# A gated mix of linear attention and expert lookup: when the output weights are split, when tile 0 is counted, and the order of work in the pairs

## The chip, the cores and the metric

The kernel runs on one core of a Trainium2 chip. The metric is device time in microseconds (us) of one execution. The engines are TensorE (PE, matmuls; PEld its weight loads), VectorE (DVE), ScalarE (ACT), GpSimd (POOL) and SyncE (SP, which issues DMA transfers). Each engine works through its own queue in order; semaphores make it wait for others.

## The reference

For S = 2048 tokens x of width D = 512 the result is g a + (1 - g) b, with g = sigmoid(x . gate_w).

```
# a: linear attention, H = 32 heads of 16
q, k, v = split(x @ wqkv)
phi(y) = [softmax(y @ w_phi), softmax(-(y @ w_phi))]       # per head, 32 features
kv = sum_s phi(k)^T v ;  z = sum_s phi(k)
a  = (phi(q) kv / (phi(q) . z + 1e-6)) @ wo
# b: 256 experts = 16 x 16 keys, one expert per head
q1, q2 = halves of x @ w_q                                 # per head
e  = 16 * argmax(q1 @ k1^T) + argmax(q2 @ k2^T)
b  = sum over heads of gelu(x . u[e]) * v[e]               # softmax over one candidate is 1
```

Since every head of a token picks one of the same 256 experts, the kernel counts for each token how often each expert was picked and computes b as (count * gelu(x u^T)) @ v.

## The kernel before

**Tiles and precision.** The tokens are 16 tiles of 128 (NT = 16). All large matmuls run on pairs high + low of a rounded number: xh and xl for x, wah/wal, wbh/wbl, eh/el and so on for the weights; a product takes three matmuls (high high, high low, low high). High parts are casts (mostly ACT: x_high, L152), low parts are subtractions (x_low, L156, on DVE; Sums.low, L189, and join_end, L315, on POOL).

**Order.** The order on every engine is written by hand: the program is written in one sequence, and each engine executes its part of that sequence in order.

**First phase, keys and values.** Tiles 0 to 4 go one at a time: kproj and vproj (PE), the feature softmax (k_diffs on DVE, L115 to L121; k_exp on ACT, L267; k_sum on DVE, L271 and L272; k_mult on POOL, L276), and kvacc (PE, L283), which adds up kv and z in PSUM. From tile 5 the tiles go in pairs t = 5, 7, 9, 11, 13 with n = t + 1. For a pair the key and value projections are computed with seven block products (prod, L453) in the manner of Strassen; these need sums of the two tiles' inputs (Sums.add on POOL, L175 to L178; Sums.high on ACT; Sums.low, which writes gl and a second xl on POOL, L189). Intermediate banks are copied (pu, pv, and pk at L530: an ACT copy, which TensorE then adds on to).

In the same phase the score weights are built: score multiplies one head's wq (loaded by SP, 1 MB each, L143 and L421) with the keys (PE), and after each second head score_planes copies the result in two 16-bit planes (ACT) and SP transposes them by DMA (L299). The join puts them together again (join_tp and join_end on ACT; sl, the low part, on POOL, L315). After the last pair, tile 15 is done alone, and fold_q folds w_phi into the query weights, which come as rawq (SP).

**Second phase, queries and output.** First the sum z of the features is spread: zsum (ACT L914, POOL L915), its high and low part (t1h by ACT, t1l by DVE, L926, two arrays of the first phase that have become free), and two pairs of matmuls (z, L898 and L899), which ACT copies to zb. Then a loop over a = 0 to 14 works on four tiles at a time, n = a + 1 (scores front_s on PE; best, the argmax masks on DVE, L706 and L707; turn_eq, SP's transpose of the masks, et), a (softmax of the queries: soft_in on DVE, soft_exp on ACT L657, soft_w, the products with zb on POOL L663, soft_sum and soft_y, the sums on DVE L667 and L677, soft_b, the scales on DVE L685 to L692 and the multiplication by them on POOL L698), b = a - 1 (planes on ACT L730, transposes by SP, join on ACT L740, the count on DVE) and z = a - 2 (mid_num, the attention output oT on PE L749; num_lo; c_join and cl, the split of count times gelu, L849; back, the output matmuls po on PE, L861 and L868; store).

The count of a tile starts with mid_mask (PE, mk, from the transposed masks) and then takes some twenty small DVE steps: a prefix or (L776 to L780), two xors (L784, L786), and a bit count by shifts and adds (L794 to L805) up to the counts cf (L808). It is a Python generator; step(t, n) issues n of its steps and drain(t) the rest, so that they lie between other DVE work. Gelu parts are gelu_in (POOL L625), gelu_act (ACT L629 to L631), gelu_out (POOL L635); coef (POOL L812) multiplies the counts with gelu, and c_planes (ACT L817) and an SP transpose turn the product.

**The output weights** wo are four blocks of 128 rows. Before, they are loaded in the second phase (wo_load), cast on ACT (L980) and subtracted on POOL (L1006): blocks 0 and 1 at a = 0 into t1h and t1l, behind their use for z; blocks 2 and 3 at a = 1 into wbh and wbl, which hold the value weights until then.

Of the kernel before, what the change touches and what calls it, by code (L numbers as in the profile page):

```python
# [35 lines left out]
def mix_kernel(ctx, tc, xT, wqT, wkT, wv, wphi, wo, wq, kk, ug, ev, cst, out):  # L36
# [131 lines left out]
    class Sums:  # L168
# [11 lines left out]
        @staticmethod  # L180
        def high(t):
            for i in range(2):
                act.copy(Sums.h[i][0], rawx[t + 1 - i])
# [208 lines left out]
    def score(n, planes=True):  # L392
        nonlocal done
        for _ in range(n):
            score_w(done, raws[done])
            done += 1
            if not 4 < done < 9:
                load_wq()
# [11 lines left out]
    for t in range(5):  # L410
# [20 lines left out]
        if t == 3:  # L431
# [3 lines left out]
            Sums.low(5)  # L435
        if t < 4:
            k_exp(t)
            k_sum(t)
# [24 lines left out]
    for t in range(5, NT - 1, 2):  # L463
# [42 lines left out]
        if t == 5:  # L506
# [3 lines left out]
            join_all()  # L510
# [6 lines left out]
        score(1)  # L517
        if t == NT - 3:
            rawq = stage(wqT, "rawq")
        score(1)  # L520
# [10 lines left out]
        if t == 5:  # L531
            k_exp(t)
            k_sum(t)
            act.copy(vn, by16(e))
# [7 lines left out]
        if t + 3 < NT:  # L542
            Sums.high(t + 2)
# [4 lines left out]
        for u in more if n < NT - 4 else ():  # L548
            x_high(u)
# [301 lines left out]
    woh = [(t1h if k < 2 else wbh)[:, k] for k in range(NK)]  # L851
    wol = [(t1l if k < 2 else wbl)[:, k] for k in range(NK)]
# [40 lines left out]
    zh, zl = (m.rearrange("p k d -> p (k d)") for m in (t1h, t1l))  # L893

    def z_final():
        for s_ in halves:
            o = tr_bank("z")
            pe.matmul(o, neg, zh[:, s_], start=True, stop=False)  # L898
            pe.matmul(o, neg, zl[:, s_], start=False, stop=True)  # L899
            act.copy(zb[:, s_], o)  # L900

    def wo_load(ks):
        for k in ks:
            rawo[k] = w3.tile([P, D], F32, tag="ot", name=f"rawo{k}")
            sp.dma_start(rawo[k], wo[:, k, :])

    rawo = {}
    kvacc(NT - 2)
    act.copy(zc, acc[:, :, F])
    neg = w2.tile([P, P], F32R, name="neg", bufs=1)  # L910
# [14 lines left out]
    act.copy(zh, zsum)  # L925
    dve.tensor_tensor(zl, zsum, zh, op=ALU.subtract)  # L926
    soft_exp(0)
    front_s(1, 0)
    mid_mask(0)
    z_final()  # L930
    gelu_rest(0)
    wo_load((0, 1))
# [11 lines left out]
    for a in range(NT - 1):  # L944
# [6 lines left out]
        if a == 2:  # L951
            gelu_pre(a)
        if B:
            planes(b, 0)
            if Z:
                c_join(z)
            planes(b, 1)
            front_q(a)
        if owed:
            back(z - 1, owed)  # L960
            store(z - 1)
        if a == 1:
# [183 lines left out]
```

## Time and profile before

| | |
|---|---|
| median of three runs | 376.97 us (376.39 to 377.11) |
| the profiled execution, its own time | 376.26 us |
| its span in the profile | 374.5 us |
| granted TensorE clock | 1.0 |
| busy: PE, PEld, DVE, ACT, POOL | 365.2, 285.7, 334.1, 256.7, 206.3 us |
| instructions in the trace | 8838 |

Times within the trace count from the start of the span. Instructions of one engine overlap at their ends, so two that follow each other directly can add up to more than the time between their starts; for matmuls of 128x512 the step from one to the next is what counts. In a row of the timeline the columns are start, duration, engine, line, operation, output<-input, shapes, number merged, and in brackets the idle time of the engine just before and what ended it. In a row of the waits they are the waiting operation, what it waited for, the sum in us, the number of times and the longest.

### The profile page before, as it was taken

To read this page: it belongs to the slowest core of one execution; us is meant where nothing else is said; L and a number is where in the kernel's file an instruction comes from. 1 tells how busy PE (TensorE), PEld (TensorE's weight loads), DVE (VectorE), ACT (ScalarE), POOL (GpSimd) and SP (SyncE) were. 2 spreads that over 40 slices of the span, in tenths; PEclk is the share of its full clock that TensorE was granted. 3 is DMA by queue.
4 is the path that set the end of the run, shared out by engine and by line. 5 is a ranking of instruction groups with operands and counts; after the bars stand their busy time and mean duration, and the time that the engine had idled before them with its cause. 6 is when DMAs were issued, how large, how long until landed. Compare 5 with 4: busy or idle time off the path is not lost.

```text
span 374.5 us, 8838 instructions
## 1 busy us (share of the span) xinstructions
PE 365.2 (98%) x3443; PEld 285.7 (76%) x3443; DVE 334.1 (89%) x784; ACT 256.7 (69%) x458; POOL 206.3 (55%) x206
## 2 busy tenths in 40 slices
PE   8999999999999998999999999999999999999995
PEld 4766776667878886778888878888778888888875
DVE  4679898999877989999999999999999999999993
ACT  5576678776576674878759568677786787687741
POOL 1089989799838745844535427335445454454700
PEclk9999999999999999999999999999999999999999
DMA  7967887757981124244253242453553532532201
GB/s 273 330 243 244 302 273 188 255 170 196 265 184 35 21 68 112 45 87 97 71 86 87 70 98 60 98 80 35 113 60 82 114 70 72 115 63 65 72 31 56
DMA packets 72218, 46.67 MB, mean 125 GB/s; under 512 B 63600, under 2 KB 64496, under 8 KB 69872
## 3 DMA queue, kind: packets, MB, share of 16 engines
q1 hardware_dynamic: 71312, 45.24, 47.0%
q10 hardware_dynamic: 864, 0.87, 0.8%
q8 instruction: 27, 0.44, 0.5%
q14 instruction: 15, 0.12, 0.1%
HBM read 26.43 MB, written 4.19 MB: 82 GB/s over the span
## 4 chain that ended last, share of the span: by engine, by line
PE 76%; DVE 7%; ACT 5%; issue 4%; DMA 3%; POOL 3%; POOLq 0%; ACTq 0%; DVEq 0%
PE po L861 10%; PE s L56 6%; PE s L57 6%; PE s L58 6%; PE po L868 5%; PE pq L56 4%; PE pk L453 3%; PE pq L58 3%; PE pq L57 3%; PE ws L292 3%; PE oT L749 2%; PE pu L453 2%; PE kvacc L283 2%; PE pp L57 2%; PE pp L58 2%
## 5 line engine op out<-in xcount | busy, mean ns | idle before, releaser
L663 POOL TENSOR_TENSOR w<-d,zb 128x512 f32<-128x512 f32 x32 | 41.0, 1297 | 78.3 <-ACT d L657 78.3
L56 PE MATMUL s<-sh,xh 128*128 128x512 f32 x128 | 50.8, 397 | 0.0
L57 PE MATMUL s<-sl,xh 128*128 128x512 f32 x128 | 49.9, 390 | 0.0
L58 PE MATMUL s<-sh,xl 128*128 128x512 f32 x128 | 49.8, 389 | 0.0
L698 POOL TENSOR_TENSOR d<-d,st 128x512 f32<-128x512 f32 x30 | 31.2, 1063 | 27.6 <-DVE st L692 25.6
L657 ACT ACTIVATE d<-d 128x512 f32<-128x512 f32 x32 | 20.1, 634 | 32.9 <-DVE d L119 24.8
L276 POOL TENSOR_TENSOR d<-d,st 128x1024 f32<-128x1024 f32 x16 | 33.6, 2101 | 13.3 <-DVE st L272 9.3
L740 ACT COPY pt<-tp 128x1024 uint16<-128x1024 uint16 x28 | 36.3, 1366 | 0.0
L730 ACT COPY pl<-d 128x1024 uint16<-128x1024 uint16 x28 | 29.2, 1045 | 9.1 <-POOL d L698 9.1
L58 PEld LDWEIGHTS s<-sh,xl 128*128 128x128 f32 x128 | 24.0, 188 | 5.0
L56 PEld LDWEIGHTS s<-sh,xh 128*128 128x128 f32 x128 | 24.0, 188 | 4.7
L57 PEld LDWEIGHTS s<-sl,xh 128*128 128x128 f32 x128 | 24.1, 188 | 4.6
L56 PE MATMUL pq<-wah,xh 128*128 128x512 f32 x64 | 26.8, 418 | 0.0
L58 PE MATMUL pq<-wah,xl 128*128 128x512 f32 x64 | 25.1, 392 | 0.0
L57 PE MATMUL pq<-wal,xh 128*128 128x512 f32 x64 | 25.0, 390 | 0.0
L271 DVE TENSOR_REDUCE st<-d 128x64 f32<-128x1024 f32 x16 | 19.4, 1212 | 5.1 <-ACT d L267 4.9
L707 DVE TENSOR_TENSOR eq<-s,mx 128x512 bf16<-128x512 f32 x32 | 22.1, 692 | 1.1
L667 DVE TENSOR_REDUCE st<-d 128x32 f32<-128x512 f32 x32 | 21.6, 683 | 1.6
L267 ACT ACTIVATE d<-d 128x1024 f32<-128x1024 f32 x16 | 17.0, 1065 | 7.6 <-DVE d L121 7.6
L156 DVE TENSOR_TENSOR xl<-xr,xh 128x512 fp32r<-128x512 f32 (+2 forms) x17 | 20.7, 1239 | 1.5 <-ACT xh L152 1.4
L706 DVE TENSOR_REDUCE mx<-s 128x32 f32<-128x512 f32 x32 | 21.8, 682 | 0.0
L677 DVE TENSOR_REDUCE st<-w 128x32 f32<-128x512 f32 x32 | 20.5, 677 | 0.6 <-POOL w L663 0.5
(258 smaller groups left out, 1119.9 us busy)
## 6 DMA issues: line engine op xcount, KB each, us to landing
wq<-wq SPq DMA_DIRECT2D x16, 1024.0 KB, 5.6
xr<-xT SPq DMA_DIRECT2D x15, 256.0 KB, 3.9
y<-ot SPq DMA_DIRECT2D x15, 256.0 KB, 2.3
rawk<-wkT SPq DMA_DIRECT2D x1, 1024.0 KB, 6.0
rawq<-wqT SPq DMA_DIRECT2D x1, 1024.0 KB, 6.7
rawo<-wo SPq DMA_DIRECT2D x4, 256.0 KB, 3.7
rawu<-ug SPq DMA_DIRECT2D x2, 258.0 KB, 4.2
rawv<-wv ACTq DMA_DIRECT2D x2, 256.0 KB, 4.5
```

The lines of the kernel that those rows point to most:

```text
L56: pe.matmul(o, ah, bh, start=(first and i == 0), stop=False)
L57: pe.matmul(o, ah, bl, start=False, stop=False)
L58: pe.matmul(o, al, bh, start=False, stop=(last and i == n - 1))
L276: pool.tensor_tensor(g64(d), g64(d), b64(st[:, 128:192]), op=ALU.mult)
L663: pool.tensor_tensor(hs(e["w"], i), hs(e["ph"], i), hs(zb, i), op=ALU.mult)
L667: dve.tensor_reduce(pair(e["st"][:, 64:128])[:, :, i], hs(e["ph"], i), axis=AX.X, op=ALU.add)
L698: eng.tensor_tensor(g64(d)[:, gs_], g64(d)[:, gs_], r[:, gs_].unsqueeze(2).to_broadcast([P, 32, F]), op=ALU.mult)
L706: dve.tensor_reduce(mx, p3, axis=AX.X, op=ALU.max)
L707: dve.tensor_tensor(e["eq"][:, 512 * half:512 * half + 512].rearrange("p (h f) -> p h f", f=F), p3, mx.unsqueeze(2).to_broadcast([P, H, F] ...
L730: act.copy(pl, e["ph"][:, halves[i]].bitcast(U16).rearrange("p (c j) -> p j c", j=2))
L740: act.copy(p16[:, :, 4 * i:4 * i + 4, :], e["tp"][i].rearrange("p (j g) n -> p j g n", j=2))
L861: pe.matmul(po, a, b, start=(i == 0), stop=False)
```

## The change

It moves work and renames where it is stored; the matmuls and their order on TensorE stay as they are.

- **Output weights.** Blocks 0 and 1 are loaded before tile 15's work into buffers of the x tiles that are spare, cast on ACT (L593) and subtracted on POOL (L594) before the last k_mult. Blocks 2 and 3 come as one 512 KB load behind kvacc of tile 14. Block 2 is split at the start of the second phase into gh and gl (POOL L945), block 3 at a = 1 into the halves of wbh and wbl (POOL L988). zh and zl become two halves each, in buffers that the later transposes use.
- **Count of tile 0.** At a = 0 only the first six steps are issued (up to the xors), and best(1, 0), best(1, 1) and turn_eq(1) come before soft_y(0); soft_b(0) has no count steps in between. At a = 1 six steps come in one piece behind soft_in(1), best(2, 0) before soft_sum, and the rest of the count behind soft_sum; vproj of tile 15 and its copy, and gelu_act(1), are moved as well.
- **Pairs.** The transposes of the score planes are issued before the next loads of wq instead of behind them, and rawq behind the last of them. x_low(7) moves to tile 3, x_low(9) behind k_exp(5), the other x_low behind k_diffs(behind); x_high(9), Sums.high(7) in part, join_end(2) and score_planes(3) move around the copy pk of t = 5.

The lines behind the change in the file have other numbers: what was L663, L667, L677 is L679, L683, L693; the count's L784, L786, L794, L797 to L802 are L800, L802, L810, L813 to L818; L849, L861, L868 are L865, L877, L884.

```diff
@@ pairs
             Sums.low(5)
+            x_low(7)
...
-        for u in (t + 2, t + 3):
-            if u < NT - 1:
-                x_low(u)
         if behind:
             k_diffs(behind)
+        for u in (t + 2, t + 3):
+            if u < NT - 1 and u not in (7, 9):
+                x_low(u)
...
             k_mult(4)
-            join_all()
+            x_high(9)
...
+            join_tp(j2, tp, tj2)
...
-        score(1)
+        score(2, t > 5)
+        if t > 5:
+            load_wq()
+            load_wq()
         if t == NT - 3:
             rawq = stage(wqT, "rawq")
-        score(1)
...
         act.copy(d, b)
         if t == 5:
+            join_end(j2, tj2)
+            score_planes(3)
             k_exp(t)
+            x_low(9)
             k_sum(t)
+            Sums.high(7, (0,))
@@ tile 15
+    rawo = {k: spare(wo[:, k], f"rawo{k}", [P, D]) for k in range(2)}
...
+    for k in range(2):
+        act.copy(t1h[:, k], rawo[k])
+        pool.tensor_tensor(t1l[:, k], rawo[k], t1h[:, k], op=ALU.subtract)
     k_mult(t)
@@ second phase
+    zh, zl = ([w3.tile([P, 512], F32R, tag=tag, name=f"{n}{i}") for i in range(2)] for n, tag in (("zh", "pl"), ("zl", "tp")))
+    for i, s_ in enumerate(halves):
+        act.copy(zh[i], zsum[:, s_])
+        dve.tensor_tensor(zl[i], zsum[:, s_], zh[i], op=ALU.subtract)
     soft_exp(0)
+    act.copy(woh[2], rawo[2])
+    pool.tensor_tensor(wol[2], rawo[2], woh[2], op=ALU.subtract)
...
+        gelu_in(a)
         if a == 1:
-            v15 = vproj(NT - 1)
-        gelu_in(a)
+            pool.tensor_tensor(wol[3], rawo[3], woh[3], op=ALU.subtract)
...
         if B:
-            soft_in(a, dealt(a, b, z))
-            drain(b)
+            if a == 1:
+                for _ in gate(a):
+                    pass
+                soft_in(a)
+                step(b, 6)
+            else:
+                soft_in(a, dealt(a, b, z))
+                drain(b)
...
         soft_w(a)
+        if a == 1:
+            best(n, 0)
         soft_sum(a, 0)
         soft_sum(a, 1)
+        if a == 1:
+            drain(b)
         if a == 0:
-            step(a, 8)
-        if a < 2:
-            for k in (2 * a, 2 * a + 1):
-                pool.tensor_tensor(wol[k], rawo[k], woh[k], op=ALU.subtract)
+            step(a, 6)
+        if a != 1:
+            best(n, 0)
         if a == 0:
-            wo_load((2, 3))
-        best(n, 0)
+            best(n, 1)
+            turn_eq(n)
...
-        soft_b(a)
-        best(n, 1)
-        turn_eq(n)
+        if a == 0:
+            soft_b(a, lambda t: None)
+        else:
+            soft_b(a)
+            best(n, 1)
+            turn_eq(n)
```

On VectorE, from the writing of tile 0's scales (the last step of soft_b) to the sums of tile 1 (st is the softmax's scratch, pq the query projection, X and T the count's scratch, mx and eq the argmax), the order before is:

```order
L692 SCALAR_TENSOR_TENSOR st_1750<-st_1750,gs_1768 128x32 x2
L802 TENSOR_TENSOR T_1862<-X_1861 128x256
L706 TENSOR_REDUCE mx_1_1890<-s_1_1821 128x32
L707 TENSOR_TENSOR eq_1871<-s_1_1821,mx_1_1890 128x512
L115 TENSOR_REDUCE st_1940<-pq_1911 128x32
L621 RECIPROCAL gs_1895<-gs_1895 128x1
L803 TENSOR_SCALAR X_1861<-T_1862 128x128
L804 TENSOR_SCALAR T_1862<-T_1862 128x128
L805 TENSOR_TENSOR X_1861<-X_1861,T_1862 128x256
L808 TENSOR_TENSOR cf_1946<-X_1861 128x256
L117 TENSOR_REDUCE st_1940<-pq_1911 128x32
```

and now, from the same place:

```order
L708 SCALAR_TENSOR_TENSOR st_1760<-st_1760,gs_1778 128x32 x2
L637 RECIPROCAL gs_1892<-gs_1892 128x1
L115 TENSOR_REDUCE st_1941<-pq_1900 128x32
L117 TENSOR_REDUCE st_1941<-pq_1900 128x32
L119 TENSOR_TENSOR d_1940<-pq_1900,st_1941 128x32x16
L121 TENSOR_TENSOR d_1940<-st_1941,pq_1900 128x32x16
L810 TENSOR_TENSOR X_1946<-m_1869,m_1870 128x256
L813 TENSOR_SCALAR T_1947<-X_1946 128x256
L814 TENSOR_TENSOR X_1946<-X_1946,T_1947 128x512
L815 TENSOR_SCALAR T_1947<-X_1946 128x256
L816 TENSOR_SCALAR X_1946<-X_1946 128x256
L817 TENSOR_TENSOR X_1946<-X_1946,T_1947 128x512
```

Before, the count of tile 0 was all but done by the end of tile 1's softmax differences; now six of its steps stand together behind them.

On GpSimd, from the first gelu step of tile 0 to the products of tile 1 (w), the order before is:

```order
L625 TENSOR_TENSOR x_1806<-x_1806,px_1805 128x256
L663 TENSOR_TENSOR w_1847<-d_1749,zb 128x32x16 x2
L1006 TENSOR_TENSOR t1l<-rawo_1810,t1h 128x512
L1006 TENSOR_TENSOR t1l<-rawo_1812,t1h 128x512
L698 TENSOR_TENSOR d_1749<-d_1749,st_1750 128x512 x2
L625 TENSOR_TENSOR x_1899<-x_1899,px_1898 128x256
L663 TENSOR_TENSOR w_2047<-d_1939,zb 128x32x16 x2
```

and now, with the split of block 2 ahead of it:

```order
L945 TENSOR_TENSOR gl<-rawo_1719,gh 128x512
L641 TENSOR_TENSOR x_1824<-x_1824,px_1823 128x256
L679 TENSOR_TENSOR w_1859<-d_1759,zb 128x32x16 x2
L714 TENSOR_TENSOR d_1759<-d_1759,st_1760 128x512 x2
L641 TENSOR_TENSOR x_1896<-x_1896,px_1895 128x256
L988 TENSOR_TENSOR wbl<-rawo_1719,wbh 128x512
L679 TENSOR_TENSOR w_2044<-d_1940,zb 128x32x16 x2
```

Two subtractions have left the stretch between products and multiplications of tile 0, one now stands ahead of the products of tile 1.

On VectorE, around tiles 3 and 4 and the first pair (xr is a raw tile), the order before is:

```order
L189 TENSOR_TENSOR gl<-xr_284,gh 128x512
L271 TENSOR_REDUCE st_439<-d_438 128x64
L272 RECIPROCAL st_439<-st_439 128x64
L115 TENSOR_REDUCE st_530<-pk_516 128x32
L117 TENSOR_REDUCE st_530<-pk_516 128x32
L119 TENSOR_TENSOR d_529<-pk_516,st_530 128x32x16
L121 TENSOR_TENSOR d_529<-st_530,pk_516 128x32x16
L156 TENSOR_TENSOR xl_68<-xr_359,xh_65 128x512
L156 TENSOR_TENSOR xl_68<-xr_397,xh_65 128x512
```

and now:

```order
L189 TENSOR_TENSOR gl<-xr_284,gh 128x512
L156 TENSOR_TENSOR xl_68<-xr_359,xh_65 128x512
L271 TENSOR_REDUCE st_439<-d_438 128x64
L272 RECIPROCAL st_439<-st_439 128x64
L115 TENSOR_REDUCE st_531<-pk_517 128x32
L117 TENSOR_REDUCE st_531<-pk_517 128x32
L119 TENSOR_TENSOR d_530<-pk_517,st_531 128x32x16
L121 TENSOR_TENSOR d_530<-st_531,pk_517 128x32x16
L156 TENSOR_TENSOR xl_68<-xr_397,xh_65 128x512
```

x_low(7), the subtraction on xr_359, now stands between gl and the sums of tile 3.

More of the change, by code (lines that the diff above doesn't have):

```diff
@@ L180, in high @@
         @staticmethod
-        def high(t):
-            for i in range(2):
+        def high(t, which=(0, 1)):
+            for i in which:
                 act.copy(Sums.h[i][0], rawx[t + 1 - i])
@@ L396, in score @@
             done += 1
[L397 removed]
+            if done < 5:
                 load_wq()
@@ L849, in back_cl @@
         eng.tensor_tensor(cl, o[:, :2 * P], ch, op=ALU.subtract)
-    woh = [(t1h if k < 2 else wbh)[:, k] for k in range(NK)]
-    wol = [(t1l if k < 2 else wbl)[:, k] for k in range(NK)]
+    woh, wol = ([a[:, 0], a[:, 1], b.rearrange("p k n -> p (k n)"), c[:, 0]]
+                for a, b, c in ((t1h, gh, wbh), (t1l, gl, wbl)))
     def back_mm(t, cols=slice(0, D), bank=None):
```

49 lines of the change are left out of this document (27 added, 22 removed).

## The prediction

> **What bounds the kernel now.** I read first the busy times of the page, then the table by stage, then PE's waits.
>
> ```profile
> PE 365.2 (98%) x3443; PEld 285.7 (76%) x3443; DVE 334.1 (89%) x784; ACT 256.7 (69%) x458; POOL 206.3 (55%) x206
> ```
>
> ```profile
> 150.00:155.00 5.00, 4.65 (x40) 3.73 (x39) 4.86 (x10) 4.94 (x10) 4.82 (x4) 1.00 0.27 51
> ```
>
> ```profile
> PE mk L768 <- DMA et<-eq: 1.6, 1, 1.6
> PE pk L453 <- ACT pk L530: 1.0, 2, 0.6
> PE oT L749 <- ACT pt L740: 0.7, 1, 0.7
> ```
>
> TensorE is busy for 98% of the span. The change leaves its matmuls and their order as they were, so all that can be won is the idle time that is left. That lies in two zones: the pairs (45 to 80 us) and the start of the second phase (130 to 163 us). For the second, the row 150 to 155 (columns PE, PEld, DVE, ACT, POOL) says more than the waits do: VectorE 4.86 of 5 us, ScalarE 4.94, GpSimd 4.82. All are full at once. The end of that zone is in the timeline of TensorE and VectorE:
>
> ```profile
> 162.28 0.40 PE L868 MATMUL po<-el,ch 128*128 128x512 f32 x1
> 162.52 0.72 PE L868 MATMUL po<-eh,cl 128*128 128x512 f32 x2
> ```
>
> ```profile
> 162.03 0.42 DVE L849 TENSOR_TENSOR cl<-ctj,ch 128x256 fp32r<-128x256 f32 x1
> ```
>
> Cl of tile 0 is ready at 162.45, and TensorE takes it at 162.52, one pitch (0.23) behind the matmul before. TensorE, having lost 3 us on the way, arrives just when VectorE is done. If its waits go and VectorE is no earlier, it waits here.
>
> **The change, first zone (pairs).**
>
> ```profile
> 70.16 0.39 PE L453 MATMUL pv<-wbh,xl 128*128 128x512 f32 x1
> 71.14 0.50 PE L453 MATMUL pk<-sh,xh 128*128 128x512 f32 x1 [0.59 <-ACT pk L530]
> ...
> 74.26 0.39 PE L453 MATMUL pe<-t1l,gh 128*128 128x512 f32 x1
> 74.75 0.50 PE L453 MATMUL pe<-t1h,gl 128*128 128x512 f32 x1
> ...
> 76.00 0.40 PE L453 MATMUL pu<-ul,xh 128*128 128x512 f32 x1
> 76.46 0.50 PE L453 MATMUL pu<-uh,xl 128*128 128x512 f32 x1
> ```
>
> Matmuls of this form follow each other at 0.23 (162.28 to 162.52 above is one). What can go: 70.16 to 71.14 is 0.98, so 0.75 too much; 74.26 to 74.75 is 0.49, so 0.26; 76.00 to 76.46 is 0.46, so 0.23; and the first matmul behind each gap takes 0.50 and not 0.39, a restart of 0.11 each. Together 1.57. I expect these to go: the two x_low that stood ahead of k_diffs(6) no longer delay it, gh of t = 7 is cast earlier, and x_high(9) no longer stands ahead of the eviction pk of t = 7. The other wait for pk, at t = 5, stays: x_high(9) takes on ScalarE the place that join_end(2) leaves. With what the earlier k_diffs may give besides, 1.8 is the upper end.
>
> What is added: x_low(7) and x_low(9) in new places on VectorE.
>
> ```profile
> 44.15 0.89 DVE L189 TENSOR_TENSOR gl<-xr,gh 128x512 fp32r<-128x512 f32 x1
> ...
> 111.30 0.63 DVE L156 TENSOR_TENSOR xl<-xr,xh 128x512 fp32r<-128x512 f32 x1
> ```
>
> ```profile
> 44.45 2.39 POOL L276 TENSOR_TENSOR d<-d,st 128x1024 f32<-128x1024 f32 x1
> 46.86 1.29 POOL L189 TENSOR_TENSOR xl<-xr,xh 128x512 fp32r<-128x512 f32 x1
> 59.27 1.31 POOL L189 TENSOR_TENSOR gl<-xr,gh 128x512 fp32r<-128x512 f32 x1
> ```
>
> ```profile
> 48.41 0.39 PE L453 MATMUL pu<-uh,xl 128*128 128x512 f32 x1
> ...
> 60.63 0.50 PE L453 MATMUL pe<-t1h,gl 128*128 128x512 f32 x1
> ```
>
> The subtraction x_low takes 0.63 alone. At 45.0, behind the VectorE gl, GpSimd is in a k_mult (L276) until 46.84. Further down I show that such pairs exclude each other; then x_low(7) ends at about 47.35, GpSimd's xl can only begin there, 0.5 late, and ends at 48.63 instead of 48.15. TensorE wants it at 48.41: a stall of 0.22 and a restart of 0.11, so +0.33 (0 if they don't exclude). The delay passes on through k_sum(3) and x_low(8) to Sums.add(7), and x_low(9) meets k_mult(4): GpSimd's gl of t = 7, which ends at 60.58 just ahead of its matmul at 60.63, comes up to 0.7 late. I take half, +0.35 (0 to 0.7). First zone: -1.57 + 0.33 + 0.35 = -0.9 (-1.8 to -0.5).
>
> The raw loads behind the transposes: the transposes go out earlier, the loads of wq later by a transpose's issue, and have over 0.5 of slack; taken at nothing. Rawq is the exception (rival C); +0.1 for it.
>
> **Second zone: what goes.**
>
> ```profile
> 133.38 0.47 PE L898 MATMUL z<-t1h,neg 128*128 128x512 f32 x1
> 133.89 0.50 PE L899 MATMUL z<-t1l,neg 128*128 128x512 f32 x1
> ```
>
> Zh and zl in halves take away 0.51 - 0.23 = 0.28 and 0.11 of restart (0.4). Best(1,1) and turn_eq(1) ahead of soft_y(0) take away the wait of mk (1.6, with its restart 1.8); two subtractions and two casts less in GpSimd's and ScalarE's queues take away that of pt (0.7, with restarts 1.0). Sum 3.2: by TensorE alone the zone would end 3.2 earlier.
>
> **Second zone: VectorE.** Its instructions up to cl of tile 0 are the same, but for one subtraction (zl) in two halves; so I count only what is lost between them, before and after. What is lost shows where one form of instruction has two durations:
>
> ```profile
> 135.25 0.20 DVE L777 TENSOR_TENSOR sb<-sa 128x64 uint16<-128x64 uint16 x1
> 136.97 0.71 DVE L797 TENSOR_SCALAR T<-X 128x256 uint32<-128x256 uint32 x1
> 140.12 0.69 DVE L677 TENSOR_REDUCE st<-w 128x32 f32<-128x512 f32 x1 [0.52 <-POOL w L663]
> 141.32 1.58 DVE L798 TENSOR_TENSOR X<-X,T 128x512 uint16<-128x512 uint16 x1
> 146.81 0.64 DVE L804 TENSOR_SCALAR T<-T 128x128 uint32<-128x128 uint32 x1
> 149.36 0.68 DVE L121 TENSOR_TENSOR d<-st,pq 128x512 f32<-128x512 f32 x1
> 154.11 1.22 DVE L685 TENSOR_TENSOR st<-st 128x64 f32<-128x64 f32 x1
> 155.26 0.73 DVE L777 TENSOR_TENSOR sb<-sa 128x64 uint16<-128x64 uint16 x1
> 156.08 0.72 DVE L778 TENSOR_TENSOR sa<-sb 128x64 uint16<-128x64 uint16 x1
> 161.03 0.29 DVE L797 TENSOR_SCALAR T<-X 128x256 uint32<-128x256 uint32 x1
> 161.36 0.42 DVE L798 TENSOR_TENSOR X<-X,T 128x512 uint16<-128x512 uint16 x1
> ```
>
> ```profile
> 136.60 0.94 POOL L625 TENSOR_TENSOR x<-x,px 128x256 f32<-128x256 f32 x1 [5.11 <-ACT x L612]
> 137.50 2.59 POOL L663 TENSOR_TENSOR w<-d,zb 128x512 f32<-128x512 f32 x2
> 140.04 2.58 POOL L1006 TENSOR_TENSOR t1l<-rawo,t1h 128x512 fp32r<-128x512 f32 x2
> 144.59 2.08 POOL L698 TENSOR_TENSOR d<-d,st 128x512 f32<-128x512 f32 x2 [1.98 <-issue]
> ```
>
> L798 takes 0.42 alone and 1.58 when it begins in a GpSimd subtraction (140.04 to 142.62, two of 1.29): it ends just behind one of them. L797 begins in GpSimd's 136.60 to 137.54 and ends just behind it. Reductions and what reads PSUM (L121) show nothing of the kind. So one holds the other off for a whole instruction, in turns. Lost so, before: L797 0.42, L798 1.16, L804 at least 0.35 (against the 0.29 of L797 on twice the elements), L685 1.02 (against the 0.20 of L777, which has as many elements), L777 0.53, L778 0.52, and 0.52 of waiting for w: 4.5 us.
>
> [...]
>
> After, I walk the new order. (1) GpSimd's gl for wo (L945, 1.29 as L1006) stands over the count of tile 0: +0.5. (2) The two xor steps (L800, L802; L784, L786 before) are ready at about 136.5, when GpSimd's L641 (L625 before) starts, at 136.60. If L800 comes first, only L802 waits for L641: +0.5. If L641 comes first, L800 waits for it and L802 for a whole product (1.29) behind it: +1.6. I take 1.6, as the subtraction of (1) puts the count late. (3) The six steps L810 to L817 stand together behind L121 of tile 1: three like L798 (0.42) and three like L797 (0.29), 2.1 free. Their GpSimd company: from the writing of the scales it runs two multiplications (2.08), L641 (0.94 at most, by L625), the subtraction L988 (1.29), the products L679 of tile 1 (2.59) and L651 (as L641), some 7.5 without a break, while VectorE needs only four instructions like L121 (4 x 0.68 = 2.7 at most) before the six begin. So they start under L641 and go in turns: a rest of L641 (0.2), then 1.29 for each of the three long ones: 4.1 lost, the sixth step free. Lost after: 0.5 + 1.6 + 4.1 = 6.2. What L685, L777, L778 lost before is gone, since GpSimd then waits for cf.
>
> So VectorE's cl comes 6.2 - 4.5 = 1.7 later, at about 164.1 (I take 1.6, since zl begins a little earlier), and TensorE, which was just in time, loses 1.6 and 0.1 of restart: +1.7. The 3.2 that go become a wait for ScalarE at the first po (its xh copies stand behind plc, which waits for GpSimd's cf, which waits for VectorE's count; up to the 3.2) and a wait for cl. From there both loops run alike.
>
> **Sum.** Own time of the profiled execution 376.26 (span 374.5); -0.9 + 0.1 + 1.7 = +0.9, so 377.2. The median of the three runs, 376.97, lies 0.71 above that execution: 377.9.
>
> **Rivals.**
> A, the tie of (2) is won: 1.1 less lost; -0.9 + 0.1 + 0.6 = -0.2, so 376.8. Against: L945 in the way; for: the start is 0.1 us apart.
> B, the other side: GpSimd and VectorE miss each other, since L121 of tile 1 comes later or L988 earlier than I walked. It decides from a shift of some 3 us, by which GpSimd's row is through before L810. Then VectorE loses 0.5 to 1 and is ahead of TensorE, and the 3.2 stays won: -0.9 + 0.1 - 3.2 = -4.0, so 373.0. For it: turn-taking moves both queues and my walk is uncertain to a whole instruction at each turn; against: 4.82 of 5 us of GpSimd.
> C, rawq late. In the timeline of SP's queue it is issued ahead of the last transpose of wq, and now behind it:
>
> ```profile
> 105.59 0.33 SPq L143 DMA_DIRECT2D rawq<-wqT  x1
> 108.12 1.24 SPq L299 DMA_TRANSPOSE wtp<-wpl  x1
> ```
>
> That moves it by up to 108.12 + 1.24 - 105.59 = 3.8. TensorE did not wait for it before; if the slack covers two thirds, the rest is 1.2: 379.1. Against: the transpose itself goes out earlier now.
> D, one-input steps aren't held: then of the six only L810, L814 and L817 wait, for the rest of L641 and for one instruction each, 2.0 instead of 4.1: 375.8. [...] Against: L797's 0.71 and L804's 0.64.
>
> **Numbers.** A measurement here tells about 0.2% (0.75 us) from no change. My forecast gets 0.41, A 0.23, B 0.19, C 0.09, D 0.08. The first zone's bounds (0.9 down, 0.4 up) and the size of (3) spread the forecast over 376.6 to 378.8: 0.03 faster, 0.11 same, 0.27 slower. A: 0.07, 0.14, 0.02. B is faster, C slower, D 0.06 faster and 0.02 same. So faster 0.35, same 0.27, slower 0.38. The range 373.3 to 379.0 takes in A, D, the forecast and the slower half of B, and leaves out the other half of B and most of C.
>
> **What would show it.** Right: no wait at mk and oT, a new one of about 3 us at the first po of tile 0 for ScalarE's xh; L813 to L816 at 1 to 1.6 us; cl at 163 to 165. In the pairs L156 at 45.0 with over 2 us, and no gaps at 71, 74.7, 76.4. Wrong: L810 to L817 at 0.3 to 0.4 each (B), or a TensorE that reaches cl's matmul before 160; a wait at foldq (C); gaps in the pairs as before.

## The result: 0.9% slower, and the profile after

| kernel | median | runs | ratio to before, 95% interval |
|---|---|---|---|
| before | 377.04 us | 376.39 to 377.52, 4 | |
| after the change | 380.53 us | 379.84 to 381.17, 4 | 1.0093 [1.007, 1.0117] |

The profiled execution of the changed kernel has a span of 378.9 us, 4.4 more than before, and a mean granted clock of 0.991 where the one before had 1.000. The page's busy times and TensorE's waits:

```profile
PE 367.3 (97%) x3443; PEld 288.0 (76%) x3443; DVE 335.8 (89%) x785; ACT 256.7 (68%) x459; POOL 205.0 (54%) x206
```

```profile
PE po L877 <- ACT xh L769: 3.7, 1, 3.7
...
PE pe L454 <- POOL gl L189: 0.9, 1, 0.9
PE foldq L208 <- DMA rawq<-wqT: 0.7, 1, 0.7
```

The waits of mk, pt and pk are gone. Three others stand there: one of 3.7 us ahead of the first output matmul, one for rawq, one for gl in the pairs. TensorE's timeline at these places:

```profile
48.79 0.50 PE L454 MATMUL pu<-uh,xl 128*128 128x512 f32 x1
...
57.14 0.39 PE L454 MATMUL pk<-sh,xh 128*128 128x512 f32 x1
...
61.41 0.50 PE L454 MATMUL pe<-t1h,gl 128*128 128x512 f32 x1 [0.93 <-POOL gl L189]
...
114.37 2.06 PE L208 MATMUL foldq<-wp,rawq 32*128 32x32 f32 x64 [0.72 <-DMA rawq<-wqT]
...
117.69 0.63 PE L57 MATMUL s<-sl,xh 128*128 128x512 f32 x1
118.12 0.63 PE L58 MATMUL s<-sh,xl 128*128 128x512 f32 x1
...
161.66 0.80 PE L877 MATMUL po<-t1h,xh 128*128 128x512 f32 x1 [3.69 <-ACT xh L769]
162.25 0.63 PE L877 MATMUL po<-t1l,xh 128*128 128x512 f32 x1
```

Behind two of the waits the matmuls come every 0.43 us (117.69 to 118.12) and not every 0.23. The table by stage has the granted clock in the last column but two:

```profile
116.50:117.00 0.50, 0.50 (x3) 0.41 (x4) 0.47 (x2) 0.47 (x2) 0.00 (x0) 1.00 0.43 143
117.50:118.00 0.50, 0.50 (x2) 0.40 (x2) 0.50 (x2) 0.50 (x2) 0.41 (x1) 0.50 0.72 258
120.50:121.00 0.50, 0.50 (x6) 0.14 (x6) 0.00 (x0) 0.00 (x0) 0.50 (x2) 1.00 0.00 0
...
162.00:162.50 0.50, 0.50 (x2) 0.40 (x2) 0.47 (x2) 0.50 (x3) 0.50 (x2) 0.50 0.03 0
165.00:165.50 0.50, 0.50 (x3) 0.38 (x3) 0.47 (x2) 0.50 (x2) 0.00 (x0) 1.00 0.25 50
```

The clock is halved for about 3.4 us behind each. Since TensorE's matmuls are the same in the same order, each can be set against its counterpart: how much later it starts than before, and where that lag changes, is where the time went.

| place (time before, us) | change of the lag, us |
|---|---|
| start of the program | +0.18 (differs by up to 0.8 between profiles of kernels that start alike) |
| pairs: 48.4 and 60.6, new waits for GpSimd | +0.19 + 1.05 |
| pairs: 57.3, 71.1, 74.8, 76.5, waits that went | -0.50 - 0.97 - 0.29 - 0.35, and -0.15 behind the first |
| 114.5, rawq | +0.70 |
| 117 to 119, half clock | +1.56 |
| z and 136 | +0.15 + 0.15 |
| 148.8 mk and 155.4 oT | -1.76 - 0.78 |
| 158.6, wait for xh | +3.81 |
| 158.9 to 160.2, half clock | +1.57 |
| behind it, up to the end | -0.2 |

That adds up to +4.4. In the second phase VectorE shows what stands behind the wait for xh:

```profile
138.93 0.73 DVE L800 TENSOR_TENSOR m<-sa 128x64 uint16<-128x64 uint16 x1
139.59 1.28 DVE L802 TENSOR_TENSOR m<-sa 128x32 uint16<-128x32 uint16 x1
...
148.46 0.92 DVE L810 TENSOR_TENSOR X<-m,m 128x256 uint32<-128x256 uint32 x1
149.41 1.27 DVE L813 TENSOR_SCALAR T<-X 128x256 uint32<-128x256 uint32 x1
150.71 1.40 DVE L814 TENSOR_TENSOR X<-X,T 128x512 uint16<-128x512 uint16 x1
152.15 1.27 DVE L815 TENSOR_SCALAR T<-X 128x256 uint32<-128x256 uint32 x1
153.45 0.72 DVE L816 TENSOR_SCALAR X<-X 128x256 uint32<-128x256 uint32 x1
154.20 0.43 DVE L817 TENSOR_TENSOR X<-X,T 128x512 uint16<-128x512 uint16 x1
...
165.84 0.42 DVE L865 TENSOR_TENSOR cl<-ctj,ch 128x256 fp32r<-128x256 f32 x1
```

and GpSimd beside it:

```profile
148.35 0.74 POOL L641 TENSOR_TENSOR x<-x,px 128x256 f32<-128x256 f32 x1
149.05 1.48 POOL L988 TENSOR_TENSOR wbl<-rawo,wbh 128x512 fp32r<-128x512 f32 x1
150.50 2.76 POOL L679 TENSOR_TENSOR w<-d,zb 128x512 f32<-128x512 f32 x2
153.22 0.79 POOL L651 TENSOR_TENSOR px<-x,px 128x256 f32<-128x256 f32 x1
```

Five of the six steps end 0.15 to 0.3 us behind the end of a GpSimd instruction (149.09, 150.53, about 151.9, 153.26, 154.01; the two products of L679 are merged in one row); the sixth, behind the last of them, is free. Together they take 6.0 us instead of 2.1. The counts are late, ScalarE's plc waits for them, and its xh casts stand behind plc:

```profile
159.55 0.62 ACT L833 COPY plc<-cf 128x512 uint16<-128x512 uint16 x1 [5.03 <-POOL cf L828]
...
161.23 0.65 ACT L769 CAST xh<-oT 128x256 fp32r<-128x256 f32 x2
```

### The profile page after: what moved, and what is told of

Same layout as the page of the kernel before. It is cut to its first block, busy times and chain, and to the rows that moved or that the text cites. A ratio compares the mean times of both kernels' runs of the same rounds, so it can differ in the third digit from the quotient of the medians.

```text
span 378.9 us, 8840 instructions
## 1 busy us (share of the span) xinstructions
PE 367.3 (97%) x3443; PEld 288.0 (76%) x3443; DVE 335.8 (89%) x785; ACT 256.7 (68%) x459; POOL 205.0 (54%) x206
## 4 chain that ended last, share of the span: by engine, by line
PE 78%; DVE 9%; POOL 4%; ACT 3%; issue 3%; DMA 2%; POOLq 0%; ACTq 0%
PE po L877 11%; PE s L56 6%; PE s L57 6%; PE s L58 6%; PE pk L454 5%; PE po L884 5%; PE pu L454 4%; PE ws L292 4%; PE pq L56 4%; PE pq L58 3%; PE pq L57 3%; PE oT L765 2%; PE kvacc L283 2%; PE pe L454 2%; PE pv L454 2%
## 5 line engine op out<-in xcount | busy, mean ns | idle before, releaser
L679 POOL TENSOR_TENSOR w<-d,zb 128x512 f32<-128x512 f32 x32 | 41.1, 1302 | 76.1 <-ACT d L673 76.1
L56 PE MATMUL s<-sh,xh 128*128 128x512 f32 x128 | 51.6, 403 | 0.0
L276 POOL TENSOR_TENSOR d<-d,st 128x1024 f32<-128x1024 f32 x16 | 32.5, 2032 | 9.8 <-ACT d L267 7.9
L683 DVE TENSOR_REDUCE st<-d 128x32 f32<-128x512 f32 x32 | 21.6, 681 | 1.4
L693 DVE TENSOR_REDUCE st<-w 128x32 f32<-128x512 f32 x32 | 20.4, 676 | 0.1
```

The source lines that it names most:

```text
L56: pe.matmul(o, ah, bh, start=(first and i == 0), stop=False)
L276: pool.tensor_tensor(g64(d), g64(d), b64(st[:, 128:192]), op=ALU.mult)
L679: pool.tensor_tensor(hs(e["w"], i), hs(e["ph"], i), hs(zb, i), op=ALU.mult)
```

## The experiments

All are compared with the kernel before, run beside them on the same chip; I give the ratio. A difference between two experiments is one of medians, some of them from different chips; the kernel before had medians of 376.78 to 377.15 us beside them. Where executions of one kernel differ by whole half-clock stretches I give their mean clock: one stretch of 3.4 us lowers it by 0.0045. What a stretch costs the whole kernel differs: of the 80 executions of the kernel before that ran beside the experiments, 24 had a clock of 0.995, and their median is only 0.3 us above that of the others. The kernels from kmult_first to cand2 keep rawq ahead of the last transpose, as in rawq_first; order_only does not.

**rawq_first.** Is the late rawq, with its half clock, a part of the loss?

```diff
-        score(2, t > 5)
-        if t > 5:
-            load_wq()
-            load_wq()
         if t == NT - 3:
+            score(1)
             rawq = stage(wqT, "rawq")
+            score(1)
+        else:
+            score(2, t > 5)
+            if t > 5:
+                load_wq()
+                load_wq()
```

> The changed kernel, with one thing put back: rawq is issued between the two score steps of the last pair, ahead of the last transpose, as before the change. Theory A (the late rawq costs its wait of 0.7 us and, behind it, 3.4 us at half clock, 1.6 us): the wait at foldq and the clock drop at 117 us are gone, the median is 2.2 lower than the changed kernel's 380.53, at 378.3. Rival (the clock drops there anyway, because fold_q's small matmuls count as idle time): only 0.7 lower, 379.8, with the half clock still behind fold_q. Rival (VectorE and GpSimd set the pace from there on, so that TensorE only waits elsewhere): about 380.5.

Measured: 379.12 us (377.68 to 380.62), 1.0054 [1.0028, 1.0079]. The wait at foldq and the half clock behind it are gone (clock 1.00 from 114 to 120 us); the span of the profiled execution is 2.2 lower. The four executions with a clock of 0.994 or 0.995 took 377.68 to 378.54, as theory A has it; the four with 0.99 took 379.71 to 380.62 and have twice as much half clock, whose place this kernel's profile, at 0.995, does not show. The profiles of t1_early and l988_later, which build on this kernel, are at 0.99: in them one stretch behind TensorE's longest wait lasts 6.8 us (in t1_early the granted clock is 0.50 from 161 to 167 us). So the wait and its clock are a part, 2.2 in a profile and 1.4 in the median.

**pe_busy.** Does the half clock behind the 3.7 us matter by itself? TensorE repeats twelve matmuls instead of idling.

```diff
         proj(pq, t, wah, wal, 0, D)
+        if t == 2:
+            proj(pq, t, wah, wal, 0, D)
```

> The changed kernel, with the twelve matmuls of the query projection of tile 2 run twice into the same bank (the second time gives the same values): TensorE works for 2.8 us of the 3.7 in which it waited for xh ahead of the first po. Theory A (the half clock behind that wait adds to it): no clock drop at 161 us, the output matmuls of tile 0 at 0.23 instead of 0.43, but VectorE's cl of tile 0 (166.3 in the changed kernel) is then the next to be late, so 0.5 lower: 380.0, with a new wait for cl. Rival (nothing but the clock counts there; cl comes in time): 1.7 lower, 378.8. Rival (the clock drop has another cause than the idle time, such as the load of the matmuls that follow): the half clock stays, 380.5.

Measured: 379.85 us (378.33 to 380.37), 1.0071 [1.005, 1.0091]. TensorE at the end of the zone:

```profile
161.86 0.50 PE L879 MATMUL po<-t1h,xh 128*128 128x512 f32 x1 [1.00 <-ACT xh L771]
162.19 0.39 PE L879 MATMUL po<-t1l,xh 128*128 128x512 f32 x1
...
165.48 0.50 PE L886 MATMUL po<-eh,ch 128*128 128x512 f32 x1 [0.61 <-ACT ch L846]
```

The half clock came from the idle time: with 1.0 us of it left, the matmuls come every 0.23 and the granted clock is 1.00 from 160 to 166 us. But only 0.6 of the 1.6 us come back, since ch, which comes from the same late counts, is the next to be waited for. Theory A's size was right; it named cl, and ch is one step earlier in the same chain.

**pairs_only** and **second_only.** The change cut in two: what its diff has under "pairs", and the rest.

> The kernel before, with the pairs' part of the change alone (orders of x_low, casts, joins, raw loads behind transposes, rawq last); output weights and the count of tile 0 as before. Theory A: the pairs win 1.0, rawq loses 2.3 (wait and half clock), so 1.3 slower than before: 378.3. Rival (the half clock behind fold_q depends on a window's phase and does not come each time): between 376.7 and 378.3. Rival (the loss is all in the second phase): 1.0 faster than before, 376.0.

Measured: 376.49 us (375.76 to 378.6, twelve runs), 0.9994 [0.9977, 1.0011]. The median lies between the two rivals. As the first of them has it, the half clock comes and goes: the five executions at a clock of 1.0 took 375.8 to 377.3, the five at 0.995 took 376.1 to 378.1, the two at 0.991 took 377.6 and 378.6. The profiled one is of the last kind. It has a half clock at fold_q and one behind the wait for mk; the kernel before has that wait too, but in its profile the clock stays at 1.0 behind it:

```profile
150.22 0.36 PE L780 MATMUL mk<-wm,et 128*128 128x16 bf16 x8 [1.61 <-DMA et<-eq]
150.51 0.74 PE L283 MATMUL kvacc<-v,d 128*32 128x16 f32 x64
151.18 0.62 PE L56 MATMUL s<-sh,xh 128*128 128x512 f32 x1
151.60 0.63 PE L57 MATMUL s<-sl,xh 128*128 128x512 f32 x1
```

> The kernel before, with the other part of the change alone (output weights early and in GpSimd's idle times, z in halves, count and argmax of tiles 0 to 2 in the new order); the pairs and rawq as before. Theory A: what the trace shows from 136 us on, 2.6 slower, and 0.3 at z: 2.9 slower than before, 379.9, with the wait for xh ahead of the first po, the half clock behind it, and six count steps of tile 0 at 6 us instead of 2.1. Rival (the part wins as the waits of mk and oT go, and the loss comes from rawq alone): 1 to 3 faster than before.

Measured: 380.41 us (379.97 to 381.08), 1.0093 [1.0075, 1.0112]. Theory A held: the second part alone costs as much as the whole change, with the wait of 3.7 for xh.

**kmult_first.** In the changed kernel z is late: TensorE reaches z 1.5 us later than before, but zl ends 2.2 later. I took GpSimd's early subtractions ahead of k_mult for the cause.

```diff
     for k in range(2):
         act.copy(t1h[:, k], rawo[k])
-        pool.tensor_tensor(t1l[:, k], rawo[k], t1h[:, k], op=ALU.subtract)
     k_mult(t)
+    for k in range(2):
+        pool.tensor_tensor(t1l[:, k], rawo[k], t1h[:, k], op=ALU.subtract)
```

> Rawq_first with one thing more: on GpSimd the two early subtractions for wo (L594) stand behind the last k_mult instead of ahead of it. Theory A (they delay k_mult of tile 15, zsum and with it VectorE's zl by 0.65 us, and VectorE carries that to cl of tile 0): VectorE's count starts 0.6 earlier relative to TensorE, the waiting time of z goes, 0.6 lower than rawq_first: 378.5 (377.6 in the runs with one clock drop). Rival (the delay at z is hidden, since the zone is bound at its end by ScalarE's xh and the half clock): no change, 379.1.

Measured: 381.54 us (381.22 to 383.1), 1.0133 [1.0103, 1.0164]: 2.4 slower than rawq_first, and both theories wrong. ScalarE's timeline, of the kernel before, the changed kernel, rawq_first and this kernel:

```profile
126.48 2.47 ACT L914 ACTIVATE zsum<-cs,zc 128x128 f32<-128x128 f32 x8
```

```profile
129.06 2.46 ACT L928 ACTIVATE zsum<-cs,zc 128x128 f32<-128x128 f32 x8 [1.15 <-POOL t1l L594]
```

```profile
127.28 2.45 ACT L931 ACTIVATE zsum<-cs,zc 128x128 f32<-128x128 f32 x8 [1.15 <-POOL t1l L597]
```

```profile
130.60 2.45 ACT L932 ACTIVATE zsum<-cs,zc 128x128 f32<-128x128 f32 x8 [4.46 <-POOL t1l L599]
```

It is not k_mult that makes z late. zsum waits for the subtractions t1l, with which it shares no data: by the code, its tile is taken from the memory that the raw blocks held, and must wait until they are read. The later the subtractions, the later zsum.

**x7_back.** Is x_low(7) at tile 3 what costs 0.2 and 1.05 in the pairs?

```diff
             Sums.low(5)
-            x_low(7)
...
-            if u < NT - 1 and u not in (7, 9):
+            if u < NT - 1 and u != 9:
```

> Rawq_first with x_low(7) back at the start of the first pair. Theory A (x_low(7) at tile 3 runs into k_mult of tile 2 on GpSimd and delays GpSimd's subtractions for TensorE, 0.2 at 48.8 and 1.05 at 61.4): both stalls shrink to what the kernel before had there (0 and 0.1), 1.1 lower: 378.0. Rival (x_low(9), which stays behind k_exp(5), makes the stall at 61.4 by itself): 0.2 lower.

Measured: 378.64 us (376.96 to 380.09), 1.0046 [1.0025, 1.0066], not apart from rawq_first by the intervals. In the trace the stall at 48.8 is gone and the one at 61 shrinks from 1.0 to 0.42. X_low(9), still in its new place, takes 1.75 there and not 0.63; that it makes the rest is not shown, and in the three later kernels with this edit the stall is 0.6 to 0.8. But the profiled execution loses 1.2 again at 112 us, to a tie. VectorE, then GpSimd:

```profile
110.43 2.40 DVE L156 TENSOR_TENSOR xl<-xr,xh 128x512 fp32r<-128x512 f32 x1 [0.22 <-ACT xh L152]
```

```profile
110.36 1.93 POOL L276 TENSOR_TENSOR d<-d,st 128x1024 f32<-128x1024 f32 x1 [0.16 <-DVE st L272]
```

k_mult is 0.07 us ahead of x_low(15), which then takes 2.4 instead of 0.69.

**count_back.** The order of count, argmax and gelu at tiles 0 and 1 as before the change, the weights where the change put them.

```diff
-                soft_in(a)
-                step(b, 6)
+            soft_in(a, dealt(a, b, z))
+            drain(b)
...
         if a == 0:
-            step(a, 6)
+            step(a, 8)
...
-            soft_b(a, lambda t: None)
+        soft_b(a)
+        best(n, 1)
+        turn_eq(n)
```

> Rawq_first with the order of count, argmax and gelu of tiles 0 and 1 as in the kernel before; the output weights stay where the change put them. Theory A (the loss of the second phase comes from six count steps that stand beside GpSimd's unbroken row): the six steps take under 3 us instead of 6, VectorE's cl comes 3 to 4 us earlier, the wait for xh shrinks below 1 us and the half clock behind it goes; mk waits again, less than 1.6. 3 to 5 lower than rawq_first: 374 to 376, faster than the kernel before. Rival (any place of the count runs into the remaining subtractions L945 and L988): 1 lower at most, 378. Rival (the order of argmax and mk was worth its 1.8, so putting it back loses that): 377.

Measured: 376.71 us (375.8 to 378.93), 1.0005 [0.9985, 1.0025]: 2.4 lower than rawq_first. The second rival holds best: mk waits again (1.7) and oT too (0.7), and the count loses other turns (before, these two steps took 0.17 and 0.43):

```profile
137.20 1.28 DVE L805 TENSOR_TENSOR m<-sa 128x32 uint16<-128x32 uint16 x1
138.52 1.46 DVE L813 TENSOR_TENSOR X<-m,m 128x256 uint32<-128x256 uint32 x1
```

**three_back** is the sum of kmult_first, x7_back and count_back.

> Kmult_first, x7_back and count_back in one. Theory A: their gains add up, since each takes away a wait of its own zone: 0.6 + 1.1 + 3 to 5, so 372.5 to 374.5. Rival (count_back takes VectorE off the end of the zone, so kmult_first adds nothing there): 0.6 more.

Measured: 379.12 us (378.83 to 381.31), 1.0082 [1.0051, 1.0114]. It carries kmult_first's loss: z waits 2.9 for zh, and 2.4 over count_back.

**l988_later.** The price of one turn: one GpSimd subtraction is taken away from beside the six steps, VectorE's order stays.

```diff
-        if a == 1:
-            pool.tensor_tensor(wol[3], rawo[3], woh[3], op=ALU.subtract)
...
             gelu_out(b)
+            if a == 1:
+                pool.tensor_tensor(wol[3], rawo[3], woh[3], op=ALU.subtract)
```

> Rawq_first with one GpSimd subtraction (block 3 of wo, 1.3 us) moved from ahead of the products of tile 1 to behind gelu_out of tile 0, where GpSimd waits for the counts; VectorE's order stays. Theory A (each of the six count steps that meets a GpSimd instruction waits for that instruction to end): one turn less is lost, the six steps take about 5 us and not 6.0, cl is 0.9 to 1.3 earlier: 378.0. Rival (the durations of the six steps come from something else than GpSimd): they stay at 6.0, 379.1.

VectorE in this kernel, whose lines are three further than the change's:

```profile
147.69 0.30 DVE L816 TENSOR_SCALAR T<-X 128x256 uint32<-128x256 uint32 x1
148.02 0.42 DVE L817 TENSOR_TENSOR X<-X,T 128x512 uint16<-128x512 uint16 x1
148.48 0.29 DVE L818 TENSOR_SCALAR T<-X 128x256 uint32<-128x256 uint32 x1
148.81 1.42 DVE L819 TENSOR_SCALAR X<-X 128x256 uint32<-128x256 uint32 x1
150.27 1.40 DVE L820 TENSOR_TENSOR X<-X,T 128x512 uint16<-128x512 uint16 x1
```

With nothing on GpSimd the steps take 0.3 and 0.4, the same steps that took 1.27, 1.40 and 1.27; the next two meet the products at 148.78 and take 1.4. Six steps: 4.75 instead of 6.0, as theory A has it. The time does not follow: 379.35 us (378.6 to 381.02), 1.0066 [1.0037, 1.0096]. ScalarE shows why:

```profile
153.51 2.52 ACT L759 COPY pt<-tp 128x1024 uint16<-128x1024 uint16 x2 [3.34 <-POOL wbl L1047]
```

pt waits for the subtraction wbl, with which it shares no data either: by the code, again a tile in the memory of a raw block that has not been read yet. oT is 2.4 late by it, and behind that wait the clock is halved for 6.8 us. The change had the subtraction early for a reason that its place alone doesn't tell.

**t1_early.** The casts of blocks 0 and 1 earlier on ScalarE, so that the subtractions, and zsum, come earlier.

```diff
         act.copy(eh[:, k, :], rawe[k])
+    for k in range(2):
+        act.copy(t1h[:, k], rawo[k])
     next(fq)
...
     for k in range(2):
-        act.copy(t1h[:, k], rawo[k])
```

> Rawq_first with ScalarE's two casts for blocks 0 and 1 of wo ahead of the last part of fold_q and k_exp of tile 15, so that GpSimd's subtractions of them can begin at 124 instead of 124.7. Theory A (the eight activations of zsum wait for these subtractions, since their tile lies where the raw blocks were; kmult_first showed that wait at 4.5 us, rawq_first has 1.15): that wait shrinks by 0.7, zl and the count come 0.7 earlier, 0.7 lower: 378.4. Rival (the raw blocks land too late, ScalarE's queue stops for them ahead of fold_q's casts): 0.5 to 1 slower.

Measured: 379.37 us (378.2 to 381.25), 1.0053 [1.0035, 1.0071]; no change by the median. In the trace zsum waits 0.60 instead of 1.15 and the lag of z falls by 0.5, but the same execution lost the tie at x_low(15) (2.40 us) and 1.4 with it. Inconclusive by itself.

**best_early.** VectorE's small steps where GpSimd has nothing to do: the argmax of tile 1, which reads PSUM, beside GpSimd's products; the count in soft_b(0), and none behind soft_in(1).

```diff
                 soft_in(a)
-                step(b, 6)
...
-        if a == 0:
-            step(a, 6)
         if a != 1:
             best(n, 0)
         if a == 0:
             best(n, 1)
             turn_eq(n)
+            step(a, 6)
...
-        if a == 0:
-            soft_b(a, lambda t: None)
-        else:
-            soft_b(a)
+        soft_b(a)
+        if a > 0:
             best(n, 1)
```

> Rawq_first with VectorE's order changed at tiles 0 and 1: the argmax of tile 1 right behind soft_sum(0), while GpSimd computes its products, the first six count steps behind it, the next five within soft_b(0), where GpSimd has nothing to do, and none behind soft_in(1). Theory A (VectorE's count steps cost what GpSimd instruction stands beside them): the steps L813 to L819 (X and T) take their free 0.3 to 0.4 each, cl of tile 0 comes 2 to 3 us earlier, the wait of TensorE for xh at the first po shrinks to about 1 us and the half clock behind it goes: 2.5 lower, 376.6. Rival (the scales of tile 0, which come 1.8 later, delay GpSimd's multiplication, the planes and their transposes, so that the wait moves to oT): no change or slower, 379 to 380.

```profile
143.83 0.42 DVE L813 TENSOR_TENSOR X<-m,m 128x256 uint32<-128x256 uint32 x1
144.30 0.29 DVE L816 TENSOR_SCALAR T<-X 128x256 uint32<-128x256 uint32 x1
144.66 0.42 DVE L817 TENSOR_TENSOR X<-X,T 128x512 uint16<-128x512 uint16 x1
145.26 0.23 DVE L818 TENSOR_SCALAR T<-X 128x256 uint32<-128x256 uint32 x1
145.72 0.29 DVE L819 TENSOR_SCALAR X<-X 128x256 uint32<-128x256 uint32 x1
```

Measured: 375.0 us (374.48 to 376.93), 0.9959 [0.9942, 0.9975]: faster than before, and 4.1 lower than rawq_first, where 2.5 was expected. These steps take their free time, TensorE no longer waits for xh, the mean clock is 0.998 to 1.0 in all ten executions. VectorE is not free of turns: three other steps of the count still take 1.17, 1.28 and 0.65 us, so it loses some 2.4 where the changed kernel loses 6.1.

**cand1** is best_early with l988_later, t1_early and x7_back.

> Best_early with l988_later, t1_early and x7_back. Theory A: VectorE no longer is the last at cl; TensorE keeps the 1.0 of the pairs, 0.8 of x_low(7), and at least half of the 3.2 of the second phase: 373.5 to 375, faster than the kernel before. Rival (x_low of tile 15 then loses its turn against k_mult, as in x7_back's trace, 1.2): 375 to 376.

Measured: 377.15 us (376.26 to 379.26), 1.0009 [0.999, 1.0028]; wrong. oT waits 3.1 us for pt, the wait that l988_later brought.

**best_k13.** The tie of x_low(15) decided: k_mult of tile 13 behind the last sl on GpSimd.

```diff
-        k_mult(t)
+        if t < NT - 3:
+            k_mult(t)
...
     join_end(j6, tj6)
+    k_mult(NT - 3)
```

> Best_early with k_mult of tile 13 moved on GpSimd behind the join of the last score weights (sl). In the traces x_low of tile 15 and this k_mult become ready within 0.1 us of each other (110.75 and 110.76 in rawq_first, where x_low is first; 110.43 and 110.36 in x7_back, where k_mult is and x_low takes 2.4 us and TensorE waits 1.2 at pk). Theory A (turns of GpSimd and VectorE, here decided by a tie): x_low always takes 0.7, the wait at pk never comes, 0.5 to 1.3 lower than best_early's 375.0: 374.2. Rival (what the first phase wins is lost again in the second, where VectorE is the last): no change, 375.0.

Measured: 375.09 us (374.23 to 375.98), 0.9946 [0.9927, 0.9965]. x_low(15) takes 0.69 and pk does not wait; the span is 372.4 against 374.3 in the profiles. The median is the same as best_early's, the ratio 0.13% lower with overlapping intervals: not settled by itself.

**cand2** is best_k13 with t1_early and x7_back.

> Best_k13 with t1_early and x7_back. Theory A: two more waits go, 0.5 at z and 0.6 to 0.8 at 61 us: 373.0. Rival (VectorE's chain from tile 0's softmax to cl is the last in the second phase and gains only the part of t1_early): 373.7.

Measured: 373.54 us (373.34 to 373.58), 0.9898 [0.9875, 0.992]: faster than both kernels, and all four executions within 0.25 us. That is between the two expectations, nearer to the rival's.

**order_only.** The changed kernel with best_early's order alone, rawq late.

> The changed kernel with best_early's order of VectorE alone (rawq stays behind the last transpose). Theory A (the loss of the change lies in two places, rawq and VectorE's count steps): what is left is the wait for rawq, 0.7, with the half clock behind it in part of the runs (0 to 1.6), so 0.7 to 2.3 over best_early: 376.5, about as the kernel before. Rival (with VectorE the last in the second phase, the late rawq is hidden): 375.0.

Measured: 375.95 us (374.62 to 376.89), 0.9962 [0.9945, 0.998]. Three executions at a clock of 0.995 took 376.64 to 376.89, the seven at 0.998 to 1.0 took 374.62 to 376.59. The profiled one, with 0.5 of waiting for rawq, is of the first kind, as the clock of its row shows:

```profile
115.00:125.00 10.00, 10.00 (x261) 8.35 (x258) 5.56 (x9) 5.79 (x10) 7.29 (x7) 0.83 0.20 56
```

This one edit to VectorE's order turns the change from 1.0093 to 0.9962. The late rawq is visible in the trace and small in the ratio (best_early, without it, has 0.9959).

## Why the prediction was right or wrong

The size was wrong: 377.9 with a range up to 379.0, measured 380.53. The direction was the likeliest named, but at 0.38 for slower and 0.35 for faster it was hardly a choice.

In the profiled execution the sum gave +0.9 us and the trace has +4.4. Two terms failed.

1. **Rawq**, put at +0.1, cost 2.26: 0.70 of waiting and 1.56 of half clock behind it.
2. **The second zone**, put at +1.7, cost 2.9. Zl came 0.65 late where the sum had it a little early, and the restart behind TensorE's new wait, put at 0.1, was a half clock of 1.57, of which pe_busy gives back 0.6.

The pairs came out within some 0.1. By medians the miss is 2.6, and there the second zone weighs more: second_only alone loses as much as the whole change, and rawq_first gives back 1.4. By its steps:

- **VectorE and GpSimd in turns**: right in mechanism. Lost after, predicted 0.5 + 1.6 + 4.1 = 6.2; measured 0.6 at L793, 1.6 at L800 and L802 (0.73 and 1.28 against 0.22 and 0.17), 3.9 at the six steps: 6.1. That the six steps came so near is in part luck. Each of the three long turns cost 0.98 and not 1.29, because the step's own time is spent anyway; L641 cost 0.50 and not 0.2, and L651 held a fifth step for 0.43, which the sum did not have. The tie of L800 went as forecast, rival A fell. L988_later shows the turns with one instruction taken away, and that steps with one input are held as well (L819, 1.42 against 0.29; in the changed kernel L813 and L815, 1.27 against 0.29), so rival D, for which no row spoke, fell.
- **The step "zl begins a little earlier"** failed: zl came 0.65 later, measured against the softmax of tile 0 ahead of it. The early subtractions hold zsum, by the code through memory: later subtractions made its wait 4.46 (kmult_first), earlier ones 0.60 (t1_early); I had looked for what reads their result, not for what is put in the place of their input.
- **"TensorE loses 1.6 and 0.1 of restart"** was mis-sized: VectorE's cl came 3.8 later than before. Of that 1.5 was the lag with which TensorE reached the zone (rawq's 2.26 less what the pairs won), 0.65 zl, 1.6 the turns.
- **The 3.2 that were to go**: 2.2 went. Mk and oT gave 1.76 and 0.78 as forecast or nearly, but z, where 0.4 was to be won, cost 0.3.
- **The restart** was taken as 0.11 everywhere. Behind 3.7 us of idle time it is a half clock of 3.4 us, 1.6 us of lag; pe_busy gives back 0.6 of it, since ch is late anyway. The clock was at 1.00 in the rows of the prediction, which priced no stretch at half clock.
- **Rival C**, at 0.09, happened, with 0.7 of waiting where I put 1.2, and with 1.6 of half clock that I did not put. In rawq_first's profile going back is worth 2.2, in its median 1.4. I had set it low because the transpose goes out earlier; it went out at 106.6 instead of 108.1, and rawq at 108.9 instead of 105.6.
- **Pairs**: the sum was right (-0.9 forecast, about -1.0 in the trace), the terms less so: the wait at 57.3, which I left standing, went (-0.65), and gl at 60.6 was 1.05 late where I took 0.35 with 0.7 as the bound.
- **The wait for xh** at the first po was foreseen with its chain; "up to 3.2" was 3.7.

Rival B, the other side, did not come by the change, but best_early shows it was within reach of VectorE's order: the five steps that were held, begun 4.6 to 7.7 us earlier, are free. Not shown: where the second half of the half clock lies in rawq_first's slower executions, and why some waits of 0.5 to 1.7 us bring one and others don't. In the trace's record of the clock the changed kernel's stretches between two changes are 3.41, 40.96 and 215.04 us, whole multiples of 3.413 (1, 12 and 63). So the clock changes on a grid in this trace; that its phase decides, as the first rival of pairs_only has it, was a guess of mine that no run shows.

## What to carry to other kernels

When every engine of a stage is near full, removing a wait of the bottleneck engine only helps if the engine that is just in time behind it gets faster too; count what that engine loses in the new order, step by step. In this kernel the count's steps on SBUF tiles are the ones to put where GpSimd is idle (five of them took 0.72 to 1.40 us each beside GpSimd in the changed kernel, 0.23 to 0.42 in best_early), and those that read PSUM or reduce can go beside it: in the changed kernel the steps of tile 1's argmax took 0.68 and 0.69 us beside GpSimd's products (140.79, 141.50) and 0.69 with GpSimd idle (142.83), and the two sums of a tile took 1.27 with it idle (143.43) and, in the kernel before, 1.27 beside its subtractions (152.66). Look for pairs that become ready within 0.1 us of each other and decide them by the order. Before moving a last reader, ask which later tile is given its memory (zsum, by the code such a tile, waited 4.46 us in kmult_first); and price a new TensorE wait at its length plus a possible half clock (1.6 us of lag behind the 3.7 us here).

## What the runs showed of the hardware that I had not expected

- The granted clock halves for 3.4 us, in two profiles for 6.8 us, behind idle time of TensorE: in all five profiles with a wait of 3.6 to 3.7 us, in the two with 2.9 and the two with 2.4, but not behind kmult_first's 2.3; in one of three behind 1.6 us with small matmuls (mk, kvacc) after it; and in all four behind 0.5 to 0.7 us with 2 us of fold_q's 32x32 matmuls after it, though by the mean clock not in every execution of these kernels. A 128x512 matmul then takes 0.43 from start to start, not 0.23.
- GpSimd and VectorE hold each other off in turns: VectorE steps of 0.3 to 0.4 us that met a run of GpSimd instructions each ended 0.15 to 0.3 us behind the end of one of these (they took 0.92, 1.27, 1.40, 1.27, 0.72), and 0.07 us decide over 1.7 us (x_low(15) takes 0.69 in rawq_first, where k_mult beside it takes 2.49, and 2.40 in x7_back, where k_mult takes 1.93).
